# Moving batch 1's rounds, two tail steps and half of a weight cast in a hand-ordered attention and gated-MLP kernel

## The chip, the cores and the metric

The kernel runs on one core of a Trainium2 chip. The metric is the device time of one execution in microseconds. The times shown are medians over several runs of the same kernel; the profile is one execution, recorded by the hardware profiler.

The engines are named as in the profile: PE is TensorE, DVE VectorE, ACT ScalarE, POOL GpSimd, SP SyncE. Each works through its own list of instructions in order. PEld is TensorE's weight load. SPq and ACTq are transfers issued from SP's and ACT's queues.

## The reference

Attention over 8 batches, 8 heads, 576 positions and a head size of 64, with a mask in blocks of 64, followed by a gated two-layer network on all 4608 rows:

```python
scores = scale * np.matmul(q, k.transpose(0, 1, 3, 2))
mask = (pos[:, None] // 64) >= (pos[None, :] // 64)
scores = np.where(mask, scores, -1e9)
attn = softmax(scores)                        # over the last axis
attn_out = np.matmul(attn, v)                 # (8, 8, 576, 64)
x = attn_out.transpose(0, 2, 1, 3).reshape(4608, 512)
out = (np.maximum(x @ w_gate, 0) * (x @ w_val)) @ w_out   # 512 -> 1536 -> 512
```

Inputs and output are float32 in device memory. The kernel multiplies in bf16.

## The kernel before

**Two streams of TensorE work.** Each batch's 512 main positions are one tile of the network; the last 64 positions of all batches (the tails) make a ninth tile. For one tile the generator `ffn_gen` issues 144 products of 128 x 128 by 128 x 512, one at a time: for each of 12 blocks of the hidden layer four products for the gate and four for the value (positions 0 to 95), then 48 for the output. Tiles 0 and 1 take some of these in another order, and tile 0 splits its output: eight blocks into two partial sums, which DVE copies out (L645), and the last four added later (L656). ACT makes `gate_sb` from the gate (L578), DVE multiplies it by the value into `hT` (L583), DVE copies the outputs (L659), and ACT's queue stores them (L554).

Between these products stands the attention of the next batch. A batch has four rounds, one per pair of heads; round r belongs to batch r // 4. A round has scores (`visit`, L378), exponentials on ACT (L387 and L393) into `attnT`, zeroed corners for the mask (`corners`, L686), a product with v for each head (`head_av` or `both_av`, L491), a normalisation on DVE (L456, L457) into `xnat`, and a transpose into `xT`, either on TensorE (`to_xT_pe`, L537 and L538) or as a transfer from SP (`to_xT_dma`, L543). The tail of a batch has the same steps in `tail_at`, ending in `xtail` and a transfer into `xTt` (L485).

**Order.** Everything is in `manual_schedule`: each engine executes its instructions in the order in which the Python code issues them. `run(base, events)` sorts pairs of a position and a function, advances the generator to that position and then calls the function. So an event's position fixes where its instructions stand on every engine and in every queue. Tile 0's events have base 0, tile 1's base 144; `round_at` turns one line of positions into the events of a round. Because a queue is a list in program order, an instruction that has to wait keeps all behind it waiting.

**Batches 0 to 3 come in by float32 transfers.** SP issues loads into ten buffers named `stage`; POOL, DVE or ACT casts them to bf16. Weights come the same way (`load_w_out` and `cast_w` for `wo`, L323). The class `Early` holds these steps for one batch: `cast_qk` (L168), `cast_v` (L181), `cast_v_chunks` (L189), `cast_v_tail` (L195), `cast_tails` (L178, the last 64 positions of q and k into `q_bt` and `k_bt`). q and k must then be transposed:

- batch 1 on TensorE: `pe_mains(hp)` for the four pairs of heads (L238, with copies into `qTm` and `kTm` by DVE and ACT, L244), and `pe_tails` for the tails (L256 and L262, into `qTt` and `kTt`);
- batches 2 and 3 by transfers from SP: `transpose(hg)` into `perm` (L209), and `transpose_tails` (L217). `unpermute` (L223) copies `perm` into place on DVE and POOL.

`q_bt` and `k_bt` have two buffers each. Batch 3's `cast_tails` writes the pair that batch 1's `pe_tails` reads.

**PSUM.** Most products share three buffers named `ffnp`; `one` has one and `sc` two. A new tile of such a pool waits for the reader of the tile that had its buffer. `pe_mains` takes one `ffnp` buffer for q and one for k, and so do gate, value, heads, `to_xT_pe` and the output tiles.

**The steps around the change, with their times in the profile.** In tile 0 (its end, 36 to 66 us) batch 1 passes through casts, `pe_mains` and rounds 4 to 7; the last of the 12 wo blocks come in as `w_out[2]`, two pieces of two blocks each, the first cast by POOL, the second by DVE. In tile 1 (66 to 104 us) rounds 8 to 11 of batch 2 run, with SP's queue carrying, in this order: batch 0's `xTt`, batch 3's loads (`load_3`), batch 2's tail transposes, xT of round 8, two `perm` transposes of batch 3's first half, xT of rounds 9 and 10, two `perm` transposes of its second half, xT of round 11, batch 3's tail transposes.

POOL's order there is written by `mains_3`, which is called for the two halves of batch 3 in turn:

```python
        def mains_3(h0):
            early[3].cast_qk(h0, 4, (pool, pool))
            if h0 == 0:
                early[3].cast_tails((pool, pool))
```

Of the kernel before, what the change touches and what calls it, by code (L numbers as in the profile page):

```python
# [17 lines left out]
def kernel(  # L18
# [299 lines left out]
    def load_w_out(i):  # L318
        return load_w(wo[i], moe_w_out, 512 * i)

    def cast_w(sts, eng):
        for dst, st in sts:
            eng(dst, st)  # L323
# [40 lines left out]
    def visit(r):  # L364

        b, hp = divmod(r, 4)
        at = attnT[r % 4]
        first = psum_sc.tile([128, 2, 512], FP, name="sc")
        second = psum_sc.tile([128, 2, 512], FP, name="sc")
        third = thirds()  # L370
        for c, hh in [(c, hh) for c in (2, 0, 1, 3) for hh in range(2)]:
            where = {
                0: first[:, hh, :],
                1: second[:, hh, 0:384],
                3: second[:, hh, 384:512],
                2: third[hh],
            }
            nc.tensor.matmul(  # L378
                where[c].rearrange("p (c n) -> p c n", n=128),
                kTm[b % 2][head_of(hh), c, hp, :],  # L380
                qTm[b % 2][head_of(hh), c:4, hp, :],
                start=True,
                stop=True,
            )

        def exp(sc, lo):
            return lambda: nc.scalar.activation(  # L387
                at[:, :, lo : lo + 512], sc, AF.Exp, scale=scale
            )

        def exp_third():
            for hh in range(2):
                nc.scalar.activation(  # L393
                    at[:, hh, 1024:1280], third[hh], AF.Exp, scale=scale
                )

        return exp_third, exp(first, 0), exp(second, 512)
# [44 lines left out]
    def corners(r, zero):  # L442

        at = attnT[r % 4]
        for lo, n in ((0, 512), (896, 128)):
            two = at[64:128, :, lo : lo + 2 * n].rearrange("p g (c n) -> p g c n", c=2)
            zero(two[:, :, :, 0:64])
# [52 lines left out]
    def head_av(r, hh):  # L500
        b, hp = divmod(r, 4)
        h = 2 * hp + hh
        at = attnT[r % 4]
        if hh == 0:
            xnats[r] = sb.tile([128, 4, 128], BF, name="xnat", bufs=3)
        xnat = xnats[r]
        if b > 0 or hh == 1:
            av = psum_ffn.tile([128, 4, 65], FP, name="ffnp")
        else:
            av = psum_one.tile([128, 4, 65], FP, name="one")  # L510
        products_with_v(b, h, at[:, hh, :], av)
        normalise(xnat[:, :, 64 * hh : 64 * hh + 64], av)

    def both_av(r):

        b, hp = divmod(r, 4)
        xnats[r] = sb.tile([128, 4, 128], BF, name="xnat", bufs=3)
        for hh in range(2):
            sc = psum_sc.tile([128, 2, 512], FP, name="sc")
            av = sc[:, 0, 0:260].rearrange("q (p e) -> q p e", e=65)  # L520
            products_with_v(b, 2 * hp + hh, attnT[r % 4][:, hh, :], av)
            normalise(xnats[r][:, :, 64 * hh : 64 * hh + 64], av)
# [160 lines left out]
    dve, act, pool = nc.vector.tensor_copy, nc.scalar.copy, nc.gpsimd.tensor_copy  # L683
# [7 lines left out]
    with tc.manual_schedule(engines={E.PE, E.DVE, E.Activation, E.Pool, E.SP}):  # L691
# [57 lines left out]
        e1, e2 = Early(1), Early(2)  # L749
        e1.load_qk(0, 4)  # L750
        ffn(23)
        w_out = [load_w_out(i) for i in range(2)]
# [12 lines left out]
        cast_w(w_out[1], pool)  # L765
        e1.cast_v(0, 4, pool)
        cast_w(w_out[2][:1], pool)
        e1.cast_qk(4, 4, (pool, None))
        e1.cast_v(4, 4, pool)
        e0.cast_tails((pool, pool))  # L770
# [12 lines left out]
        def round_at(p, r, av, to_xT, after=(6, 13)):  # L783

            exps = []

            def begin():
                exps.extend(visit(r))
                exps[0]()
                exps[1]()  # L790

            return [
                (p, begin),
                (p + after[0], lambda: exps[2]()),
                (min(p + after[1], av[0] - 0.5), lambda: corners(r, zero_dve)),
                *(
                    [(av[0], lambda: both_av(r))]
                    if av[1] is None
                    else [(av[i], lambda i=i: head_av(r, i)) for i in range(2)]
                ),  # L800
                (to_xT[0], lambda: to_xT[1](r)),
            ]

        def tail_at(p, b, av):
            exps = []
            x = sb.tile([64, 512], BF, name="xtail", bufs=2)

            def begin():
                exps.extend(tail_visit(b))
                exps[0]()  # L810
                exps[1]()

            def end():
                tail_av(b, 1, x)
                tail_to_xT(b, x)

            return [
                (p, begin),
                (p + 6, lambda: exps[2]()),
                (av[0], lambda: tail_av(b, 0, x)),  # L820
                (av[1], end),
            ]
# [25 lines left out]

        def mains_3(h0):
            early[3].cast_qk(h0, 4, (pool, pool))  # L850
            if h0 == 0:
                early[3].cast_tails((pool, pool))

        def v_3():
# [8 lines left out]
        def mains_2(h0):  # L863
            e2.load_v_chunks(h0 // 4)
            e2.cast_qk(h0, 4, (pool, pool))
            e2.transpose(h0 // 4)

        def load_tails():
# [2 lines left out]
            e2.load_tails((0, 1))  # L871
            e2.load_tails((2,))

        events = round_at(101, 4, (113, 114), (117, pe_xT), (6, 11))
        events += round_at(108, 5, (120, 120.1), (128, pe_xT), (6, 11.5))
        events += round_at(128.5, 6, (139, 140), (146, pe_xT), (4, 9))
        events += round_at(138, 7, (148, None), (153, pe_xT), (3, 8))
        events += [
            (80, lambda: e1.cast_qk(0, 4, (None, dve))),
            (96, lambda: e1.pe_mains(0, (dve, act))),  # L880
            (98, lambda: e1.pe_mains(1, (dve, act))),
            (112.3, lambda: cast_w(w_out[2][1:], dve)),
            (120.2, lambda: e1.cast_qk(4, 4, (None, act))),
            (123, lambda: e1.pe_mains(2, (dve, act))),
            (125.5, lambda: e1.pe_mains(3, (dve, act))),
            (128, lambda: mains_2(0)),
            (142, lambda: e0.pe_tails((dve, act))),
            (143, lambda: mains_2(4)),
# [3 lines left out]
        events = tail_at(24, 0, (40, 44)) + tail_at(116, 1, (132, 136))  # L892
        for r, p in ((8, 41), (9, 58), (10, 75), (11, 92)):
            events += round_at(p, r, (p + 21, p + 25), (p + 25, to_xT_dma))
        events += [
            (100, lambda: e1.pe_tails((dve, act))),
            (20, lambda: store.pop()()),
            (25, un(2, 0, (dve, pool))),
            (28, un(2, 1, (dve, pool))),
# [3 lines left out]
            (56, un(2, 3, (dve, pool))),  # L903
            (60, tails_2),
            (66, lambda: mains_3(0)),
            (81, lambda: early[3].transpose(0)),
            (82, lambda: mains_3(4)),
            (101, lambda: early[3].transpose(1)),
            (118, lambda: early[3].transpose_tails()),
# [5 lines left out]
        for b in range(3, B):  # L915
            events = tail_at(120, b, (136, 140))
# [43 lines left out]
```

## Time and profile before

| | before |
|---|---|
| median of 7 runs | 374.36 us (373.0 to 376.07) |
| the profiled execution, its own time | 373.0 us |
| its span, first to last instruction | 370.8 us |
| PE busy | 357.0 us (96%) |
| DVE, ACT, POOL busy | 173.9, 169.8, 111.1 us |
| granted TensorE clock | 0.995 of full speed |
| moved by transfers | 51.35 MB, 138 GB/s |

PE's idle time by stretch, from the windows view:

| stretch, us | PE busy, us | PE idle, us |
|---|---|---|
| 0 to 20 | 16.39 | 3.61 |
| 20 to 40 | 19.96 | 0.04 |
| 40 to 60 | 17.95 | 2.05 |
| 60 to 80 | 19.84 | 0.16 |
| 80 to 100 | 19.74 | 0.26 |
| 100 to 120 | 16.76 | 3.24 |
| 120 to 140 | 19.95 | 0.05 |
| 140 to 160 | 19.27 | 0.73 |

In a line of the profile, the tile written stands left of the arrow and the tile read right of it; L numbers are lines of the kernel. A line of the timeline gives start, length, engine, line, operation, tiles and a count; brackets at its end give the idle time of the engine just before it and what ended that time. A line of the waits gives total, count and longest, in us. In the slices each digit is a fortieth of the span in tenths of busy time.

### The profile page before, as it was taken

The page shows a single profiled execution, that of the slowest core. Times are in us where ns is not written, and L with a number is a line of the kernel's source. Part 1 is how long each engine was busy: PE and PEld are TensorE (multiplying, and loading weights), DVE is VectorE, ACT ScalarE, POOL GpSimd, SP SyncE. Part 2 cuts the span into 40 slices and gives each one's busy share as a digit, 9 for nine tenths or more (in the row PEclk, how much of TensorE's full clock was granted, in tenths as well). Part 3 has the DMA queues.
Part 4 walks back from the last instruction along what each step waited for, and adds up shares of the span by engine and source line. Part 5 has one row for each costly group of instructions (what it writes and reads, how often), then busy time and mean ns, then how long its engine had stood idle before and what let it go on. Part 6 is the DMA issues. An engine that isn't in the chain of part 4 may idle for free.

```text
span 370.8 us, 7469 instructions
## 1 busy us (share of the span) xinstructions
PE 357.0 (96%) x2963; PEld 176.9 (48%) x2963; DVE 173.9 (47%) x399; ACT 169.8 (46%) x278; POOL 111.1 (30%) x141
## 2 busy tenths in 40 slices
PE   6999989999969999999999999999999999999996
PEld 2644445445534545444554455444544454444443
DVE  4744475675534644454345533554354443423432
ACT  4833646667335662456445544553465323302310
POOL 6675635282379920940066004000000000000000
PEclk9899999999999999999999999999999999999999
DMA  8999999999879999997499857875200320020014
GB/s 256 292 348 360 297 244 325 206 214 248 133 156 119 128 131 181 166 125 147 110 95 134 122 128 85 53 80 135 80 17 14 63 82 7 0 87 28 0 36 108
DMA packets 145187, 51.35 MB, mean 138 GB/s; under 512 B 124544, under 2 KB 139136, under 8 KB 145152
## 3 DMA queue, kind: packets, MB, share of 16 engines
q1 hardware_dynamic: 83616, 34.62, 43.8%
q0 software_dynamic: 56256, 7.08, 40.7%
q10 hardware_dynamic: 5280, 9.18, 7.7%
q8 instruction: 23, 0.38, 0.5%
q14 instruction: 12, 0.10, 0.1%
HBM read 37.75 MB, written 9.44 MB: 127 GB/s over the span
## 4 chain that ended last, share of the span: by engine, by line
PE 86%; DMA 6%; DVE 3%; ACT 3%; issue 1%; POOL 1%; SPq 0%; ACTq 0%; DVEq 0%; POOLq 0%
PE ffnp L568 49%; PE ffnp L625 21%; PE ffnp L491 4%; DMA xT<-xnat 3%; PE sc L378 3%; PE ffnp L471 2%; DMA perm<-k_bf 2%; PE one L378 1%; PE ffnp L238 1%; DMA perm<-q_bf 1%; PE ffnp L679 1%; PE sc L335 1%; PE sc L412 1%; ACT gate_sb L578 1%; DVE hT L583 1%
## 5 line engine op out<-in xcount | busy, mean ns | idle before, releaser
L583 DVE TENSOR_TENSOR hT<-gate_sb,ffnp 128x512 bf16<-128x512 bf16 x106 | 72.7, 686 | 95.5 <-PE ffnp L568 82.6
L578 ACT ACTIVATE gate_sb<-ffnp 128x512 bf16<-128x512 f32 x108 | 64.7, 601 | 105.9 <-PE ffnp L568 105.7
L568 PE MATMUL ffnp<-xT,wg 128*128 128x512 bf16 x384 | 103.9, 380 | 4.4 <-DMA xT<-xnat 3.9
L625 PE MATMUL ffnp<-wo,hT 128*128 128x512 bf16 (+1 forms) x444 | 102.5, 374 | 0.7 <-DVE hT L583 0.4
L568 PE MATMUL ffnp<-xT,wv 128*128 128x512 bf16 x376 | 100.2, 380 | 0.0
L568 PEld LDWEIGHTS <-wv 128*128 128x128 bf16 x432 | 39.9, 98 | 49.3 <-issue 5.7
L568 PEld LDWEIGHTS <-wg 128*128 128x128 bf16 x432 | 40.2, 98 | 47.6 <-issue 5.0
L625 PEld LDWEIGHTS <-hT 128*128 128x128 bf16 x444 | 40.5, 98 | 42.0 <-issue 1.3
L387 ACT ACTIVATE attnT<-sc 128x1024 bf16<-128x1024 f32 x56 | 56.9, 1041 | 0.0
L659 DVE COPY ob<-ffnp 128x512 f32<-128x512 f32 (+1 forms) x35 | 23.7, 676 | 40.1 <-PE ffnp L625 40.1
L276 POOL DMA_DIRECT2D v_bf<-in_v_dram x20 | 16.8, 879 | 68.8 <-PE ffnp L471 68.8
L491 PEld LDWEIGHTS <-attnT 128*128 128x128 bf16 x640 | 26.1, 98 | 15.1 <-DVE xnat L457 3.5
L456 DVE RECIPROCAL recip<-ffnp 128x4 f32<-128x4 f32 (+1 forms) x73 | 13.0, 179 | 32.9 <-PE ffnp L491 21.0
L491 PE MATMUL ffnp<-v_bf,attnT 128*128 128x65 bf16 x570 | 26.6, 194 | 0.8 <-DVE attnT L686 0.8
L393 ACT ACTIVATE attnT<-one 128x256 bf16<-128x256 f32 x28 | 10.7, 384 | 32.4 <-PE ffnp L378 29.3
L457 DVE TENSOR_TENSOR xnat<-ffnp,recip 128x256 bf16<-128x256 f32 x57 | 24.2, 424 | 2.5 <-DMA xT<-xnat 0.6
L433 ACT ACTIVATE attnTt<-one 64x256 bf16<-64x256 f32 x8 | 3.0, 377 | 34.0 <-PE ffnp L412 32.6
L378 PE MATMUL sc<-qTm,kTm 64*128 64x512 bf16 (+1 forms) x168 | 17.2, 305 | 0.2 <-ACT attnT L387 0.2
L378 PEld LDWEIGHTS <-kTm 64*128 64x128 bf16 x224 | 9.3, 94 | 16.2 <-issue 12.3
L424 ACT ACTIVATE attnTt<-sc 128x1024 bf16<-128x1024 f32 x16 | 15.6, 1016 | 0.0
L276 POOL DMA_DIRECT2D k_bf<-in_k_dram x16 | 14.3, 932 | 0.7 <-DMA v_bf<-in_v_dram 0.4
L276 POOL DMA_DIRECT2D q_bf<-in_q_dram x16 | 14.4, 953 | 0.0
(87 smaller groups left out, 260.3 us busy)
## 6 DMA issues: line engine op xcount, KB each, us to landing
out_dram<-ob ACTq DMA_DIRECT2D x32, 256.0 KB, 2.8
stage<-in_moe_w_gate_dram SPq DMA_DIRECT2D x6, 512.0 KB, 9.1
stage<-in_moe_w_val_dram SPq DMA_DIRECT2D x6, 512.0 KB, 8.8
stage<-in_q_dram SPq DMA_DIRECT2D x6, 512.0 KB, 6.5
stage<-in_k_dram SPq DMA_DIRECT2D x6, 512.0 KB, 7.6
stage<-in_moe_w_out_dram SPq DMA_DIRECT2D x6, 512.0 KB, 9.2
stage<-in_v_dram SPq DMA_DIRECT2D x20, 128.0 KB, 5.4
stage<-in_v_dram SPq DMA_DIRECT2D x8, 256.0 KB, 6.5
```

The costliest lines, as they stand in the source:

```text
L276: nc.gpsimd.dma_start(dst, src[b, :, 128 * c : 128 * c + n, :].rearrange("h p d -> p h d"),)
L378: nc.tensor.matmul(where[c].rearrange("p (c n) -> p c n", n=128), kTm[b % 2][head_of(hh), c, hp, :], qTm[b % 2][head_of(hh), c:4, hp, :], ...
L387: return lambda: nc.scalar.activation(at[:, :, lo : lo + 512], sc, AF.Exp, scale=scale)
L424: return lambda: nc.scalar.activation(at[:, :, 2 * i : 2 * i + 2, 0:256], main[i].rearrange("p g (h n) -> p g h n", h=2), AF.Exp, scale=scale,
L456: nc.vector.reciprocal(recip, av[:, :, 64])
L457: nc.vector.tensor_tensor(out=out, in0=av[:, :, 0:64], in1=recip.to_broadcast([rows, n, 64]), op=AX.mult,)
L491: nc.tensor.matmul(av[:, p, :], at[:, col : col + 128], v_bf[b % 2][:, c, h, :], start=(p == 0), stop=(c == p), skip_group_check=True,)
L568: nc.tensor.matmul(to, (wg, wv)[t][f // 4][:, c, 128 * (f % 4) : 128 * (f % 4) + 128], x[:, c], start=(c == 0), stop=(c == 3),)
L578: nc.scalar.activation(gate_sb, gate, AF.Relu)
L583: nc.vector.tensor_tensor(out=h, in0=gate_sb, in1=val, op=AX.mult)
L625: nc.tensor.matmul(op, hT[f][:, 128 * s : 128 * (s + 1)], wo[f // 4][:, f % 4, n0:n1], start=(f == lo), stop=(f == hi - 1),)
L659: nc.vector.tensor_copy(ob, op)
```

## The change

It has three parts.

1. In tile 1 batch 1's `pe_tails` stands at position 88 instead of 100, and batch 3's `cast_tails` follows the casts of its second half instead of its first. SP's order of transfers stays the same.
2. In tile 0 `pe_mains(0)` and `pe_mains(1)` move from 96 and 98 to 93 and 95, round 4 begins at 96 instead of 101 and round 5 at 104 instead of 108. Round 4's corners are zeroed at 107 instead of 112, its heads stand together at 112, and its xT at 116. Round 5's heads move from 120, ahead of `pe_mains(2)` and `pe_mains(3)`, to 127, behind them, and its xT from 128 to 131, behind the scores of round 6. `pe_mains(3)` moves from 125.5 to 125.
3. The last piece of wo (two blocks, 1024 columns) is cast in halves: one block by POOL, ahead of the cast of batch 1's second half of q, and one by DVE, between the normalisations of round 4's two heads.

```diff
         cast_w(w_out[2][:1], pool)
+        last_w = [[a[:, c : c + 1] for a in w_out[2][1]] for c in range(2)]
+        cast_w(last_w[:1], pool)
         e1.cast_qk(4, 4, (pool, None))
...
         def mains_3(h0):
             early[3].cast_qk(h0, 4, (pool, pool))
-            if h0 == 0:
+            if h0 == 4:
                 early[3].cast_tails((pool, pool))
...
-        events = round_at(101, 4, (113, 114), (117, pe_xT), (6, 11))
-        events += round_at(108, 5, (120, 120.1), (128, pe_xT), (6, 11.5))
+        events = round_at(96, 4, (112, 112.1), (116, pe_xT), (6, 11))
+        events += round_at(104, 5, (127, 127.1), (131, pe_xT), (6, 15))
         events += round_at(128.5, 6, (139, 140), (146, pe_xT), (4, 9))
         events += round_at(138, 7, (148, None), (153, pe_xT), (3, 8))
         events += [
             (80, lambda: e1.cast_qk(0, 4, (None, dve))),
-            (96, lambda: e1.pe_mains(0, (dve, act))),
-            (98, lambda: e1.pe_mains(1, (dve, act))),
-            (112.3, lambda: cast_w(w_out[2][1:], dve)),
+            (93, lambda: e1.pe_mains(0, (dve, act))),
+            (95, lambda: e1.pe_mains(1, (dve, act))),
+            (112.05, lambda: cast_w(last_w[1:], dve)),
             (120.2, lambda: e1.cast_qk(4, 4, (None, act))),
             (123, lambda: e1.pe_mains(2, (dve, act))),
-            (125.5, lambda: e1.pe_mains(3, (dve, act))),
+            (125, lambda: e1.pe_mains(3, (dve, act))),
...
         events += [
-            (100, lambda: e1.pe_tails((dve, act))),
+            (88, lambda: e1.pe_tails((dve, act))),
             (20, lambda: store.pop()()),
```

## Prediction

> **What bounds the kernel now.** I read the busy line and the slices first, then the waits, then the chain, then the timeline of the two stretches that the change touches.
>
> ```profile
> PE 357.0 (96%) x2963; PEld 176.9 (48%) x2963; DVE 173.9 (47%) x399; ACT 169.8 (46%) x278; POOL 111.1 (30%) x141
> PE   6999989999969999999999999999999999999996
> PE ffnp L568 <- DMA xT<-xnat: 3.9, 3, 3.2
> POOL q_bt L178 <- PE ffnp L256: 7.0, 1, 7.0
> ```
>
> TensorE is busy for 357.0 of 370.8 us. From 160 us to 320 us the windows show it busy without a gap, so only its holes can be won: 3.6 us in the first 20 us and 3.8 us in the last 51 us (neither touched), 2.05 us between 40 and 60 us (tile 0's end), and 3.24 us between 100 and 120 us. The last is one wait, the first product of tile 2 that needs round 11's block of xT. The change works on both middle holes. The 7.0 us for which POOL waits on batch 1's tail transposes is what its tile 1 half takes away, so the question is whether that wait leads to the 3.24 us. The timeline answers (start, length, engine, line):
>
> ```profile
> 75.72 0.42 DVE L457 TENSOR_TENSOR xtail<-ffnp,recip 64x256 bf16<-64x256 f32 x1
> 76.16 1.58 SPq L485 DMA_TRANSPOSE xTt<-xtail  x1
> 94.72 1.03 POOL L168 CAST k_bf<-stage 128x1024 bf16<-128x1024 f32 x1
> 95.38 1.26 SPq L209 DMA_TRANSPOSE perm<-q_bf  x1
> 96.73 1.28 SPq L209 DMA_TRANSPOSE perm<-k_bf  x1
> 98.11 4.38 SPq L543 DMA_TRANSPOSE xT<-xnat  x2
> 102.59 1.26 SPq L209 DMA_TRANSPOSE perm<-q_bf  x1
> 103.94 2.19 SPq L209 DMA_TRANSPOSE perm<-k_bf  x1
> 106.23 1.63 SPq L543 DMA_TRANSPOSE xT<-xnat  x1
> 109.41 0.38 PE L568 MATMUL ffnp<-xT,wg 128*128 128x512 bf16 x1 [3.24 <-DMA xT<-xnat]
> ```
>
> The transposes at 95.38 and 96.73 take batch 3's first half, cast by 85.58. Those at 102.59 and 103.94 take the second half, which POOL finished at 95.75, 6.8 us before SP came to it. SP had no free moment: from 71.98 to 107.86 its instructions follow each other within about 0.13 us. The last xT block was ready at 98.47 (DVE) and stood in that queue until 106.23. So the hole comes from the queue, not from POOL. The chain of waits does run through POOL's casts, but there it joins the cast that ends at 95.75 to the transpose issued at 96.73, which takes the other half.
>
> What starts this queue matters more. SP finishes its previous load at 76.04; the transpose at 76.16 waits for DVE's xtail, which ends at 76.14. So SP alone could start 0.12 us sooner, no more, while any delay of TensorE before tile 1's position 44 delays xtail, this transpose and, in order, all that follows up to 109.41. Time won before position 44 only lengthens the hole; time lost there reaches the end.
>
> **Part 1, batch 3's tail casts and batch 1's tail transposes.** Order on SP is unchanged. On POOL the two second-half casts come ahead of the two tail casts, and pe_tails moves from position 100 to 88, from 92.23 to about 88.1. The second-half loads were issued at 80.31 and 81.03; with the page's medians of 6.5 and 7.6 us they land near 86.8 and 88.6, so the casts (1.03 us each) end near 89.6 and the tails (0.61 each) near 90.8. Waiting behind them are the copies of perm at 102.48, held by a landing, and on SP the second-half transposes at 102.59 and the tail transposes at 107.95. All keep over 6 us of cover, and no later load waits for the stage buffer that the tails give back later. Gain 0. On TensorE the same eight transposes run (0.4 us); their evacuations (DVE 0.28, ACT 0.37) now stand before a gate copy and round 11's exponentials, worth perhaps 0.2 us, under the 3.24 us hole. Without the hole it would cost that 0.2.
>
> A rule would read this differently. The row: a 128x1024 bf16 transpose (256 KB) is issued in 1.26 to 2.19 us and lands in 3.7 to 5.6. The Trainium skill, page "DMA: Bandwidth & Descriptors", section "Latency and other measured facts", gives DMA transposes about 261 GB/s: 1.0 us for that block, and for the 1.66 MB from 89.96 to the last xT an estimate of 6.4 us. By the rule that queue would be empty at 96.4, POOL's cast at 95.75 would set the second-half transposes, xT would follow at 98.5 and there would be no hole; a delay in tile 0 would still pass. By the trace it takes 19.4 us. The 3.2 us row decides for the trace.
>
> **Part 2, tile 0.** What holds TensorE here:
>
> ```profile
> 47.82 0.48 PE L491 MATMUL ffnp<-v_bf,attnT 128*128 128x65 bf16 x10 [0.82 <-DVE attnT L686]
> 49.17 1.04 POOL L168 CAST q_bf<-stage 128x1024 bf16<-128x1024 f32 x1 [2.92 <-DMA stage<-in_q_dram]
> 51.73 1.04 ACT L168 CAST k_bf<-stage 128x1024 bf16<-128x1024 f32 x1 [0.93 <-DVE recip L456]
> 52.84 0.40 PE L238 MATMUL ffnp<-ident,k_bf 128*128 128x128 bf16 x4 [0.20 <-ACT k_bf L168]
> 58.01 0.28 PE L378 MATMUL one<-qTm,kTm 64*128 64x256 bf16 x1
> ```
>
> I followed the new order with the durations of these rows: a 512-column product 0.215 us, four transposes 0.22, a head's ten products 0.30, a round's scores 0.65, DVE's evacuation 0.69, ACT's 0.59, about 0.45 from a product's start to its reader.
>
> Pulling pe_mains(0), (1) and rounds 4 and 5 forward adds waits: 0.4 us at the first k transposes (their PSUM buffer is that of the last gate, whose copy ends at 39.51) and 0.2 at the next. It removes the 0.41 us wait at 40.59, and the 0.82 at 47.82, since the corners of round 4 are now zeroed before the two ob copies. Round 4's first head comes to 46.3 instead of 47.82. Then come three waits on DVE of about 0.4 each (for the second ob copy, for DVE's half of the wo cast, for the second head's product), and the q transposes of pe_mains(2) come to 50.8 instead of 52.25.
>
> There the lead ends. k_bf's second half lands at 50.74 (issued 42.94, 7.8 us to landing). Ahead of its cast ACT issues an out store; before, that store waited for a later load and left at 51.33. Now it waits for this landing. So the cast runs from about 51.2 to 52.24 and the k transposes start at 52.3, against 52.84: TensorE waits 1.3 us, and of a lead of 1.5 about 0.5 is left.
>
> After it, round 5's two heads (0.6 us), which stood before this gate and beside its wait, stand behind it. From these transposes to the end of round 6's scores the new order holds 0.22+0.43+0.22+0.22+0.43+0.60+0.22+0.65 = 2.99 us of work, and 0.6 of waits (0.2 on the evacuation that also held the old order, 0.1 at the heads, 0.3 on round 5's DVE products): 55.95 against 55.74. Four transposes and ten products follow (2.37 against 2.15), so round 7 starts at 58.4 against 58.01: **0.4 us late**. Nothing from there to 76.14 gives it back: TensorE idles 0.16 us from 60 to 80. xtail, SP's queue and the last xT move by 0.4 at most. Bounds: -0.5 (the lead at the gate is kept, worth only 0.1 at the end) and +1.3 (the lead is all lost and each reader costs 0.2 more). I take +0.4, the walk's own sum.
>
> **Part 3, the last wo piece.** DVE's cast of 1024 columns takes 0.69 us. Halved, it lies between 0.35 and 0.69 on DVE; on POOL between 0.52 (half of 1.04) and 0.61 (the 128x512 cast of k_bf takes 613 ns). I take 0.4 and 0.61, by the nearest rows. The piece lands at 46.6, so POOL casts from 46.6 to 47.2 within its 2.92 us of idle time before 49.17. The q_bf cast does not move unless that cover is gone; then it would cost 0.61. DVE's half now falls between the normalisations of round 4's heads, near 48.0. It holds one wo product, the second head's product on DVE and to_xT of round 4, all ahead of the 1.3 us wait at the gate: 0. With that wait gone, about 0.3.
>
> The second rule speaks against splitting. DVE's perm copies take 0.55 us each at 99.15, with POOL idle, and 1.01 at 68.69, beside POOL's copies. The Trainium skill, page "SBUF — State Buffer", section "Who interferes with whom", says that a DVE cast in a two-port mode and GpSimd lock each other out for a whole instruction. By the rule, halves that meet cost DVE up to 0.61 us, still under the gate's 1.3. By the rows' times they miss each other by 0.8 us. Both give 0.
>
> **Sum.** 0 + 0.4 + 0 = +0.4 us on the profiled execution: its span of 370.8 becomes 371.2 and its 373.0 us (2.2 lie outside the span) 373.4. The seven runs' median is 1.36 us above that execution, so I forecast 374.36 + 0.4 = 374.8 us. About 0.3%, 1.1 us, is what a measurement of this kernel can tell from no change.
>
> **Rivals.**
> (a) The walk is right, or its lead survives: the end moves by -0.1 to +1.1 us; 374.3 to 375.4. For it: the hole absorbs gains and the gate absorbs the first half of tile 0. Chance 0.62.
> (b) POOL did hold SP, as the chain view has it: with the casts sooner the hole of 3.24 us goes in part or whole; 371.1 to 373.2. Against it: SP came to the second half 6.8 us after its cast. Or the queue's pace differs from run to run so that the hole opens less. Chance 0.10.
> (c) Slower: ACT works in order, and round 5's xT copy (0.59 us) now stands between round 6's two large exponentials (1.0 each). Round 7's second scores need the later one's PSUM buffer. If round 6's scores are later than 56.1 this holds TensorE; each further 0.1 us is then paid again in round 7's exponentials and at its corners, 0.4 to 1.0 us on top of the 0.4, all of it handed to xtail. It passes the bound once xtail ends after 77.3. 375.5 to 376.2, likeliest 375.7. For it: ACT is in use for 13.45 of the 20 us from 40 to 60. Against it: in my walk the exponential ends at 58.65, just before the scores ask for it at 58.75. Chance 0.28.
>
> That the change does not do what it says is excluded by the order of the instructions: each named move is there.
>
> **Numbers.** 0.62 + 0.28 + 0.10 = 1. The range leaves out most of (b) and the end of (c): 373.5 to 376.1.
>
> **What would show it.** Right: POOL's 7.0 us wait gone or under 3; SP's second-half transposes again over 25 us after the xTt transpose; a wait of 3 us or more on xT at tile 2's start; k transposes of pe_mains(2) near 52.3; round 7's scores at 58.2 to 58.7; the corner wait gone. Wrong: the xT wait under 2 us (then b), xtail later than 77.3 (then c), or k_bf's cast no sooner than before.

## The result, and the profile after

The changed kernel takes 374.12 us (median of 27 runs, 371.47 to 377.14), the kernel before 374.46 us (median of 64 runs, 372.44 to 376.67). The ratio, taken over the runs within 1.5% of the fastest of their kernel and not the quotient of these medians, is 0.9999, with a 95% interval of 0.9984 to 1.0014: no difference that these runs can tell. The forecast was 374.8 us, 0.4 us over the median that stood on record then, and under the 1.1 us that it took for the least that can be told.

The profiled execution of the changed kernel took 375.76 us (span 373.7), 2.8 us more than the profiled execution before, although the medians are equal. First its busy time, then the row of granted clocks in 40 slices, then the two longest waits of TensorE in the middle of the kernel.

```profile
PE 361.3 (97%) x2963; PEld 178.1 (48%) x2963; DVE 174.1 (47%) x399; ACT 169.6 (45%) x278; POOL 111.8 (30%) x142
PEclk9999999999987999999999999999999999999999
...
PE ffnp L568 <- DMA xT<-xnat: 2.9, 1, 2.9
PE ffnp L238 <- ACT k_bf L168: 1.5, 1, 1.5
```

TensorE's wait for xT is still there, 2.9 us in place of 3.2, and the gate at batch 1's k has become a wait of 1.5 us. The clock row shows what the median hides: two slices at 8 and 7 tenths, around the hole's end and behind it. The timeline of the hole's queue, after (start, length, engine, line):

```profile
77.18 0.42 DVE L457 TENSOR_TENSOR xtail<-ffnp,recip 64x256 bf16<-64x256 f32 x1
77.63 1.20 SPq L485 DMA_TRANSPOSE xTt<-xtail  x1
89.76 1.04 POOL L168 CAST k_bf<-stage 128x1024 bf16<-128x1024 f32 x1 [0.87 <-PE ffnp L568]
...
102.50 1.52 SPq L209 DMA_TRANSPOSE perm<-q_bf  x1
105.54 2.37 SPq L543 DMA_TRANSPOSE xT<-xnat  x1
...
110.48 0.59 PE L568 MATMUL ffnp<-xT,wg 128*128 128x512 bf16 x1 [2.86 <-DMA xT<-xnat]
```

POOL now ends the cast of batch 3's second half of k at 90.80 instead of 95.75. SP comes to its transposes at 102.50 all the same, 11.7 us later, and xT of round 11 is issued at 105.54. The hole ends at 110.48. The queue's unbroken stretch again begins with the transpose of xTt, 0.03 us after xtail's end at 77.60.

What made this execution longer is seen in the windows over the hole (TensorE's busy time stands first; the three last columns are granted clock, transfer share and GB/s):

```profile
108.00:110.00 2.00, 0.00 (x0) 0.00 (x0) 0.00 (x0) 0.80 (x1) 0.00 (x0) 0.87 1.21 190
110.00:112.00 2.00, 1.52 (x4) 0.55 (x4) 0.00 (x0) 0.90 (x2) 1.64 (x2) 0.50 0.28 49
112.00:114.00 2.00, 2.00 (x6) 0.73 (x5) 0.69 (x1) 0.62 (x1) 2.00 (x3) 0.50 0.65 53
114.00:116.00 2.00, 2.00 (x7) 0.60 (x5) 0.00 (x0) 0.60 (x1) 2.00 (x4) 0.50 1.73 110
...
112.00:114.00 2.00, 2.00 (x28) 1.29 (x27) 0.69 (x1) 0.75 (x2) 2.00 (x3) 1.00 1.68 124
```

TensorE is granted half its clock from before the hole's end to about 116.3 us; the last line is the same stretch of before, at full clock. From 110.48 on that is 5.8 us at half speed (to the 0.92 of the window from 116 to 118), or 2.9 us lost. With the 1.07 us by which tile 2's work goes on later (110.48 against 109.41), less the 0.73 us of idle time that before had between 140 and 160 us and this execution did not, it makes 3.2 us; the spans differ by 2.9, so 0.3 us of the sum is not accounted for.

Tile 0's gate, after:

```profile
52.41 1.04 ACT L168 CAST k_bf<-stage 128x1024 bf16<-128x1024 f32 x1 [1.99 <-DMA stage<-in_k_dram]
53.51 0.40 PE L238 MATMUL ffnp<-ident,k_bf 128*128 128x128 bf16 x4 [1.54 <-ACT k_bf L168]
59.67 0.28 PE L378 MATMUL one<-qTm,kTm 64*128 64x256 bf16 x1
```

This execution was already 0.79 us late at the last value products of tile 0 (L568 with `wv`, first at 39.50 against 38.71), ahead of all that the change moves. Batch 1's second half of k landed near 51.9 us instead of 50.7: it was issued at 43.01 and took 8.9 us, before 42.94 and 7.8. From the k transposes to round 7's scores it takes 6.16 us.

### The profile page after: what moved, and what is told of

Same layout as the page of the kernel before. It is cut to its first block, busy times and chain, and to the rows that moved or that the text cites. A ratio compares the mean times of both kernels' runs of the same rounds, so it can differ in the third digit from the quotient of the medians.

```text
span 373.7 us, 7467 instructions
## 1 busy us (share of the span) xinstructions
PE 361.3 (97%) x2963; PEld 178.1 (48%) x2963; DVE 174.1 (47%) x399; ACT 169.6 (45%) x278; POOL 111.8 (30%) x142
## 4 chain that ended last, share of the span: by engine, by line
PE 84%; DMA 11%; ACT 2%; POOL 1%; issue 0%; DVE 0%; SPq 0%; ACTq 0%; POOLq 0%
PE ffnp L568 45%; PE ffnp L625 23%; DMA stage<-in_moe_w_val_dram 5%; PE ffnp L491 4%; PE sc L378 3%; DMA stage<-in_moe_w_out_dram 3%; PE ffnp L471 3%; DMA stage<-in_k_dram 2%; PE one L378 1%; DMA xT<-xnat 1%; ACT attnT L351 1%; PE sc L412 1%; PE ffnp L679 1%; PE ffnp L238 1%; PE sc L335 0%
## 5 line engine op out<-in xcount | busy, mean ns | idle before, releaser
L568 PE MATMUL ffnp<-xT,wg 128*128 128x512 bf16 x384 | 104.9, 383 | 3.2 <-DMA xT<-xnat 2.9
L568 PE MATMUL ffnp<-xT,wv 128*128 128x512 bf16 x376 | 102.3, 385 | 0.0
L568 PEld LDWEIGHTS <-wv 128*128 128x128 bf16 x432 | 40.3, 98 | 49.6 <-issue 7.2
L568 PEld LDWEIGHTS <-wg 128*128 128x128 bf16 x432 | 40.4, 98 | 48.2 <-issue 6.6
L223 POOL COPY kTm<-perm 128x512 bf16<-128x512 bf16 x8 | 9.3, 1181 | 19.5 <-DMA perm<-k_bf 13.8
```

The costliest lines, as they stand in the source:

```text
L568: nc.tensor.matmul(to, (wg, wv)[t][f // 4][:, c, 128 * (f % 4) : 128 * (f % 4) + 128], x[:, c], start=(c == 0), stop=(c == 3),)
```

## The experiments

All were compared with the kernel before on the same chip; its medians in the four groups were 374.5 (runs 1 to 4), 374.8 (5 to 8), 374.54 (9 to 11) and 374.65 us (12). The theory to be tested was the prediction's: the hole is made by SP's queue, so part 1 is worth nothing, what happens in TensorE's order ahead of xtail passes through whole, and tile 0's gate eats the lead. The rivals were that POOL's 7.0 us wait makes the hole, and that the tile 0 order is worth more, either way, than the walk gave.

| run | kernel | median, us | ratio to before, 95% | runs at granted clock 0.994 or less |
|---|---|---|---|---|
| | before (all four groups) | 374.5 to 374.8 | | 66 of 134 |
| | after | 374.12 | 0.9999, 0.9984 to 1.0014 | 15 of 27 |
| 1 | before, second-half transposes later | 372.78 | 0.9947, 0.9923 to 0.9971 | 0 of 14 |
| 2 | after, the same | 372.12 | 0.9945, 0.9919 to 0.9971 | 0 of 10 |
| 3 | part 1 alone | 374.79 | 1.0011, 0.9989 to 1.0033 | 10 of 14 |
| 4 | parts 2 and 3 alone | 374.24 | 0.9992, 0.9972 to 1.0012 | 14 of 22 |
| 5 | before, work ahead of xtail | 377.32 | 1.0065, 1.0037 to 1.0092 | 2 of 7 |
| 6 | before, the same work behind it | 371.93 | 0.9939, 0.9918 to 0.9960 | 1 of 18 |
| 7 | run 1, batch 4's transposes earlier | 370.23 | 0.9878, 0.9841 to 0.9914 | 0 of 6 |
| 8 | run 2, round 5's heads first | 372.37 | 0.9936, 0.9911 to 0.9962 | 5 of 15 |
| 9 | run 2, batch 4's transposes earlier | 370.07 | 0.9887, 0.9855 to 0.9918 | 2 of 6 |
| 10 | part 3 alone | 374.22 | 1.0004, 0.9985 to 1.0023 | 7 of 22 |
| 11 | run 9, round 5's heads first | 370.06 | 0.9882, 0.9856 to 0.9908 | 1 of 6 |
| 12 | run 6 with half the work | 374.05 | 0.9981, 0.9957 to 1.0006 | 9 of 22 |

**Runs 1 and 2: take the queue out of the way.** The two transposes of batch 3's second half move on SP behind xT of round 11, in the kernel before and in the changed one. Their copies, which read the result, move to tile 2.

```diff
-            (101, lambda: early[3].transpose(1)),
+            (118, lambda: early[3].transpose(1)),
...
-                events.append((2, un(3, 2, (dve, pool))))
+                events.append((20, un(3, 2, (dve, pool))))
```

> The kernel before with one reordering in SP's queue: the two perm transposes of batch 3's second half stand behind xT of round 11 (position 118 of tile 1 instead of 101), and their unpermute at position 20 of tile 2 instead of 2. Queue theory: xT of round 11 is issued at about 102.6 us instead of 106.2 and lands near 105.7, before TensorE asks for it at 106.2; the wait of 3.2 us on xT at tile 2's start falls under 0.5 us and the time falls by 2.5 to 3.5 us, ratio 0.991 to 0.993. POOL theory (POOL's wait on batch 1's tail transposes holds the queue): POOL's casts end where they did, so the hole stays near 3 us and the ratio is 1.000.

> The changed kernel with the same reordering. Queue theory: the hole is gone here too, and with it the mask over tile 0: what tile 0's new order costs is now seen whole, so this is slower than the kernel before with the reordering by what the walk gave, 0.4 us (ratio to before 0.992 to 0.994). If tile 0's new order had gained time that the hole swallowed, this is the faster of the two, by up to 1 us.

Measured: 372.78 and 372.12 us. In the first, POOL's wait on the tail transposes has kept its full length (from the waits on POOL), while the three xT blocks of rounds 9 to 11 leave SP one behind the other (from the timeline):

```profile
POOL q_bt L178 <- issue: 7.0, 1, 7.0
...
98.78 4.91 SPq L543 DMA_TRANSPOSE xT<-xnat  x3
```

Tile 2's product with round 11's xT starts in run 1 without a wait:

```profile
106.94 0.39 PE L568 MATMUL ffnp<-xT,wg 128*128 128x512 bf16 x1
```

So the hole of 3.24 us is gone in both profiles: the queue made it, and POOL's wait did not. The gain of 2.0 us by the ratio (1.7 by the medians) is under the forecast 2.5 to 3.5 us, since a part moved on: at tile 3's start, 147 to 150 us, run 1 waits three times for xT, 1.7 us in all against 0.6 before, and the granted clock falls to 0.57 from 150 to 154 us. The two kernels differ only by the change under study, and their intervals lie on each other: with the hole gone it still brings and costs nothing that can be told. The 0.4 us by which run 2 was to be the slower does not show, and these intervals do not exclude it.

**Runs 3 and 4: the halves of the change.** Run 3 has part 1 alone (the tails), run 4 parts 2 and 3 alone (tile 0 and the wo halves); so each takes over some lines of the change and leaves the others as they were:

```diff
-            if h0 == 0:                                   # run 3
+            if h0 == 4:
-            (100, lambda: e1.pe_tails((dve, act))),
+            (88, lambda: e1.pe_tails((dve, act))),
...
-        events = round_at(101, 4, (113, 114), (117, pe_xT), (6, 11))       # run 4, and so on
+        events = round_at(96, 4, (112, 112.1), (116, pe_xT), (6, 11))
```

> The kernel before with the two tail steps of tile 1 alone (pe_tails at 88, batch 3's cast_tails after the second half's casts). Queue theory: POOL's wait of 7.0 us goes, the second-half casts end near 89.6 instead of 95.75, SP issues the second-half transposes at 102.6 as before and the hole stays at 3.2 us: ratio 1.000, within 0.001. POOL theory: the hole shrinks by 2 us or more, ratio 0.994 or less.

> The changed kernel with the two tail steps of tile 1 put back: tile 0's new order and the split wo cast alone. The walk: POOL's wait of 7.0 us back, round 7's scores 0 to 0.6 us later than before relative to the landing of the second half of k, ratio 1.000 to 1.002. If the new order gained and the gain was given back by the tail steps, the ratio is 0.998 or less.

Measured: 374.79 and 374.24 us, both the same as before within 0.3%. The first product of tile 2 in run 3, and the gate of tile 0 in run 4:

```profile
109.57 0.38 PE L568 MATMUL ffnp<-xT,wg 128*128 128x512 bf16 x1 [3.32 <-DMA xT<-xnat]
```

```profile
51.74 0.40 PE L238 MATMUL ffnp<-ident,k_bf 128*128 128x128 bf16 x4 [1.42 <-ACT k_bf L168]
57.91 0.28 PE L378 MATMUL one<-qTm,kTm 64*128 64x256 bf16 x1
```

Run 3 has no wait of POOL on the tail transposes, and the hole is 3.32 us: part 1 does what it says, and it is worth nothing. Run 4 has the gate's 1.42 us, and 6.17 us from there to round 7. Its round 7 starts 7.76 us after the landing of k's second half (issued at 43.05, 7.1 us to landing), against 7.27 before: 0.5 us later, as forecast.

**Runs 5 and 6: the same work ahead of the queue's start and behind it.** `junk(10)` issues ten products of 512 columns that nobody reads, about 2.15 us of TensorE (10 x 0.215). Run 5 puts them at position 31 of tile 1, ahead of xtail; run 6 at position 61, behind it.

```diff
         events += [
+            (31, lambda: junk(10)),      # run 5;  run 6: (61, ...)
             (100, lambda: e1.pe_tails((dve, act))),
```

> The kernel before with ten 512-column matmuls of no use (about 2.15 us of PE) at tile 1's position 31, ahead of batch 0's tail (its xtail is written at position 44). Queue theory: SyncE's unbroken stretch begins with that tail's transpose, so it and the 3.2 us hole of round 11's xT move along with PE: hole again 3.0 to 3.5 us, transpose of xTt some 2 us later than in before, and the whole loses all of it: +2.1 us, 376.3 to 376.8 beside 374.5, ratio 1.005 to 1.006. Rival (the hole's end is set by something that does not follow PE, a load or GpSimd's chain): the hole takes the 2.1 us up and shrinks to about 1.1 us, ratio 0.999 to 1.001. Third (the lost time is the clock's, not the wait's): ratio anywhere, the hole unchanged, and the granted clock decides.

> The same ten matmuls at tile 1's position 61, behind that tail. Queue theory: SyncE has begun its stretch already and does not wait for PE in it, so the 2.1 us are taken from the hole: 1.0 to 1.4 us of it left, ratio 0.999 to 1.001 (374.1 to 374.9). It is the test of the prediction's statement that between the tail and tile 2 PE's gains and losses are worth nothing. Rival (the hole follows PE, since round 9's or 10's xnat is what SyncE waits for): hole 3.2 us still, ratio 1.005 to 1.006 as for the other.

Measured: 377.32 us, 0.65% slower, and 371.93 us, 0.6% faster, for the same added work. Run 5's queue start and hole:

```profile
79.16 1.65 SPq L485 DMA_TRANSPOSE xTt<-xtail  x1
...
112.34 0.38 PE L568 MATMUL ffnp<-xT,wg 128*128 128x512 bf16 x1 [2.77 <-DMA xT<-xnat]
```

xTt left 3.0 us later than in before and the end of the hole came 2.9 us later: what TensorE loses ahead of xtail passes to the end. (2.15 us of the 3.0 are the added work; this execution was also 1.2 us late at round 7, ahead of it.) That is the prediction's rule, and the rival (a hole whose end stands still) is out. Run 6 went further than any of the theories stated for it. In its profile no wait for xT is left at all:

```profile
100.00:120.00 20.00, 20.00 (x213) 10.46 (x210) 12.36 (x25) 8.89 (x15) 16.90 (x20) 1.00 1.49 145
```

The time from the start of xTt's transfer to TensorE going on with round 11's xT is the measure of the queue. It was 33.25 us in before (76.16 to 109.41), and lies between 32.85 and 35.33 us in the seven profiles that have the hole. With 33.25 and TensorE's arrival 32.0 us after xTt (75.71 to 107.70), 1.25 us of hole should have been left, as forecast. In run 6 the block was there when TensorE arrived, so the queue needed under 32.0 us. The median suggests that this was the rule in its runs. An estimate: without any wait for xT there run 7 below took 370.23 us, and with 2.15 us more that makes 372.4; 1.25 us of hole would have made 373.6, and run 6 measured 371.9. Why SP's queue is quicker beside this work is not known.

**Run 12: half of it.** Five products in place of ten.

```diff
-            (61, lambda: junk(10)),
+            (61, lambda: junk(5)),
```

> The sixth experiment with five of the ten matmuls (about 1.1 us of PE at tile 1's position 61). In the sixth the hole went altogether and the kernel came out 1.5 to 3.1 us faster with 2.1 us more work, where the queue theory alone had it equal. Clock theory (a wait of PE of about 3 us is followed, in near half the runs, by a stretch at a lower granted clock, which costs some 1.5 us in such a run): the hole shrinks to about 2.1 us, no run or few below a granted clock of 0.995, and the time falls by the mean cost of the dips, 0.6 us: 373.7 to 374.2, ratio 0.997 to 0.999. Queue theory alone: 374.3 to 374.7, ratio 1.000. Third (SyncE's stretch itself gets 2 us shorter when PE comes later): hole gone, ratio 0.990 to 0.993.

Measured: 374.05 us; 9 of its 22 runs had a granted clock of 0.994 or less. Its hole:

```profile
111.15 0.38 PE L568 MATMUL ffnp<-xT,wg 128*128 128x512 bf16 x1 [4.25 <-DMA xT<-xnat]
```

Here the queue took 35.33 us, the longest of all: the last xT, issued at 105.74, let TensorE go only 5.4 us later (3.2 in before). So the third theory, a queue that is always quicker when TensorE comes later, does not hold in this profile. Nor did the clock theory's hole of 2.1 us and its "no run or few" come: 9 of 22 runs are at the lower clock, about the share of before. The ratio's interval takes in the forecasts of the clock and of the queue. The run does not decide why run 6 gained more than its sum; what it shows is that the hole is no constant of the kernel: 2.8 to 4.3 us in the seven profiles that have it.

**Runs 7, 9 and 11: take away the next wait as well.** In run 1 SP stood idle from about 115 to 122 us, and then batch 4's four transposes (from 123.4 to 137.3) held the xT blocks of rounds 13 to 15. Run 7 issues these four at position 44 of tile 2, ahead of round 12's xT. Run 9 has the same two queue edits on the changed kernel. Run 11 also puts round 5's heads and xT back ahead of `pe_mains(2)`, by the edit of run 8 below.

```diff
-                events.append((66, lambda b=b: dma_transposes(b + 1)))
+                events.append((44 if b == 3 else 66, lambda b=b: dma_transposes(b + 1)))
```

> The kernel before with batch 3's second-half transposes at tile 1's position 118 (the first experiment), and with batch 4's transposes at tile 2's position 44 in place of 66, so ahead of round 12's xT on SyncE. Queue theory: SyncE stood idle from about 115 to 122 us there, and batch 4's four transposes then held round 13's and 14's xT until 137; issued sooner, they leave the queue free sooner, and the 1.7 us of waits for xT at 147 to 151 us go: 371.0 to 372.2, ratio 0.991 to 0.994. Rival (batch 4's rows have not landed by then, so SyncE waits for them with round 12's xT behind it): the waits stay at 1.5 us or more, 372.5 to 373.5.

> The changed kernel with the two queue edits that took the waits for xT away (batch 3's second-half transposes at tile 1's position 118, batch 4's transposes at tile 2's position 44): no wait for xT is left to hide what the change does to tile 0 and to the tails. Prediction's steps (tile 0 +0.4 us, tails and halves 0): 370.2 + 0.4 = 370.6, range 369.9 to 371.3, ratio to before 0.987 to 0.991, no wait for xT of over 0.5 us, granted clock 0.995 or above. Rival (the hole had hidden a gain of the change): 368.9 to 369.8, ratio under 0.987. Other rival (it had hidden a loss): 371.5 or more.

> The changed kernel with those two queue edits and round 5's heads ahead of batch 1's second half (the order of the eighth experiment). Prediction's step that the heads behind the gate cost 0.4 to 1.0 us of tile 0: 0.4 to 1.0 us under the ninth run, 369.5 to 370.2, ratio 0.985 to 0.988, PE busy 18.4 us or more in 40 to 60. Rival (order there is worth nothing): equal to the ninth run within 0.3 us.

Measured: 370.23, 370.07 and 370.06 us, 1.1 to 1.2% faster than before. In run 7 batch 4's first transpose leaves at 117.01 in place of 123.39, and all four xT blocks of batch 3 start from 130.06:

```profile
117.01 4.67 SPq L286 DMA_TRANSPOSE qTm<-q_bf  x1
...
130.06 11.51 SPq L543 DMA_TRANSPOSE xT<-xnat  x4
```

TensorE is then busy for 39.95 of the 40 us in the windows from 100 to 120 and from 140 to 160. Run 7 came out 0.8 us faster than its forecast's lower end (371.0). That forecast took 1.7 us of waits off run 1; run 1's profile also has 3.4 us at half clock at tile 3's start, worth up to 1.7 us, which run 7's has not. That these are the 0.8 us is likely, not shown. Run 9 answers the question that the hole had kept open: with no wait for xT to hide behind, the change again makes no difference (0.9887 against 0.9878, intervals nearly the same). Neither rival of run 9 came, though two of its six runs had a clock under the 0.995 that it was to keep; a tile 0 effect of 0.4 us is below what these intervals tell. Run 11's 370.06 us fits both its forecast (369.5 to 370.2) and its rival (run 9 within 0.3 us), so the time does not decide. Its sign failed: TensorE is busy for 16.66 us between 40 and 60, not 18.4 or more, because a product waited 1.96 us for POOL (run 10 below).

**Run 8: round 5's heads ahead of the gate.** On the kernel of run 2:

```diff
-        events += round_at(104, 5, (127, 127.1), (131, pe_xT), (6, 15))
+        events += round_at(104, 5, (120, 120.1), (122.5, pe_xT), (6, 15))
```

> The changed kernel with the second-half transposes at position 118 (the second experiment), and with round 5's two heads and its xT back ahead of batch 1's second half (tile 0's positions 120, 120.1 and 122.5 in place of 127, 127.1 and 131). Prediction's step: with the heads behind the gate round 7's scores come 6.1 us after the k transposes of pair 2; with them ahead of it the gate's wait falls from 1.5 us to under 0.6, and round 7 comes 5.0 to 5.4 us after them, so 0.4 to 1.0 us of tile 0 is won: 371.2 to 371.9, ratio 0.991 to 0.994. Rival (PE is filled anyway and the order there is worth nothing): within 0.1% of the second experiment, 371.8 to 372.5.

Measured: 372.37 us, beside 372.12 of run 2: nothing won that can be told. Its ratio of 0.9936 lies in the forecast's range and also within 0.1% of run 2's, so the time does not decide; the trace says more. The order did as expected on the spot: the wait on k's cast is gone, and round 7's scores (58.59) come 4.94 us after the k transposes (53.65). But these now stand behind the heads and xT, with a wait of 0.51 us for DVE's xnat and 0.23 for ACT's copy of xT ahead of them, and round 7 starts no sooner than in the other profiles of either order (57.4 to 59.7). In this profile the work was only moved to the other side of the gate.

**Run 10: the wo halves alone.** The kernel before with part 3.

```diff
+        last_w = [[a[:, c : c + 1] for a in w_out[2][1]] for c in range(2)]
+        cast_w(last_w[:1], pool)
...
-            (112.3, lambda: cast_w(w_out[2][1:], dve)),
+            (112.3, lambda: cast_w(last_w[1:], dve)),
```

> The kernel before with the last wo piece's second part cast in two halves, one on GpSimd and one on VectorE, and nothing else of the change. Prediction's step: hidden, 0: ratio 0.998 to 1.002, 374.0 to 375.2, the hole of 3 us as in before. Rival (GpSimd's cast in tile 0 delays batch 1's k cast or VectorE's order at the gate): +0.4 to +0.8 us, ratio 1.001 to 1.002, not to be told by the time, but k's transposes of pair 2 in tile 0 would wait 0.4 us or more longer than in before (0.2 us there).

Measured: 374.22 us, ratio 1.0004. Its gate in tile 0 waited all the same, and in run 11 a product waited for POOL's half:

```profile
53.85 0.40 PE L238 MATMUL ffnp<-ident,k_bf 128*128 128x128 bf16 x4 [1.56 <-ACT k_bf L168]
```

```profile
49.03 0.59 PE L625 MATMUL ffnp<-wo,hT 128*128 128x512 bf16 x2 [1.96 <-POOL wo L323]
```

The time says 0, as forecast. The sign that its rival named does show, a gate wait of over 0.4 us. But what released ACT's cast of k there, at 52.75, was the landing of k itself, 9.1 us after its issue and after 2.46 us of waiting, not POOL or DVE, and run 7, which has no halves, waited 0.54 us at this gate. So the halves did not delay the cast; the late landing did.

## Why the prediction was right

**The hole (the first term, 0).** Shown. The queue makes it: moving two transposes out of its way took the hole away with POOL's wait untouched (run 1); removing POOL's wait left 3.32 us (run 3). Work ahead of xtail passes on (run 5), work behind it does not (runs 6 and 12). One statement was too strict: that xtail starts the queue. In ten of the fourteen profiles xTt leaves within 0.12 us of xtail's end. In runs 3, 9, 10 and 11 SP's own last load ended later, and xTt left 0.46, 1.19, 1.07 and 1.26 us after xtail; a delay of TensorE up to that size would have passed nothing on there. Run 9, whose xtail ended at 76.36:

```profile
75.53 1.92 SPq L158 DMA_DIRECT2D stage<-in_v_dram  x1
77.55 1.23 SPq L485 DMA_TRANSPOSE xTt<-xtail  x1
```

The trace's pace of SP's transposes was the right one to use. The Trainium skill's "DMA: Bandwidth & Descriptors", section "Latency and other measured facts", with its 261 GB/s, would have had no hole by the prediction's estimate; in the eight profiles with this order SP took 27.9 to 30.3 us from xTt to the issue of round 11's xT.

**Tile 0 (the term of +0.4).** The corner wait and the hT wait are gone in all profiles of the change's order (after and runs 2, 4 and 9). Run 9 tests the walk best, since its execution comes to tile 0's end as the one before did: the last value products start at 38.71 in both, and k's second half lands near 50.7 in both (42.83 + 7.9 and 42.94 + 7.8). Before, and then run 9:

```profile
38.71 1.03 PE L568 MATMUL ffnp<-xT,wv 128*128 128x512 bf16 x4
```

```profile
38.71 0.38 PE L568 MATMUL ffnp<-xT,wv 128*128 128x512 bf16 x1
52.27 0.40 PE L238 MATMUL ffnp<-ident,k_bf 128*128 128x128 bf16 x4 [1.25 <-ACT k_bf L168]
58.44 0.28 PE L378 MATMUL one<-qTm,kTm 64*128 64x256 bf16 x1
```

The walk had the k transposes at 52.3 after a wait of 1.3 us and round 7 at 58.4; measured are 52.27, 1.25 and 58.44, against 58.01 before: +0.43 us, by the mechanism that was named. The parts were less exact. Waits that were put at 0.4 us came out at 0.17 to 0.28. The written terms (52.3 + 2.99 + 0.6 + 2.37) make 58.26, so 58.4 holds 0.14 us that are not named.

But +0.4 belongs to that execution and is no constant. Where the gate waits (after, runs 4 and 9), the new order starts round 7 between 7.7 and 7.8 us after k's landing. Run 2 came to its last value products at 41.00, k was there, and round 7 started at 59.38, 18.38 us later. The old order needs 19.25 or 19.26 us for the same way in runs 3, 5, 6 and 12, and 19.30 before. So the new order is the longer one where k lands late beside TensorE, and the shorter one, by 0.9 us in this single profile, where it does not. On average over the profiles, from the first of these products to round 7, the old order (before and runs 1, 3, 5, 6, 7, 10, 12) and the new one (after and runs 2, 4, 9) both take 19.5 us. An average effect of tile 0 on the time is therefore not shown. The landing is what the walk took as fixed: it took 6.6 to 9.1 us from issue, in no clear relation to the order.

**Part 3 (0).** Right in the time (run 10). The reason given was too good: the piece "lands at 46.6" in one execution, but in run 11 both halves waited for it until about 48.1 and a product waited 1.96 us for POOL's. Round 7 came there 20.61 us after the first of the last value products, against 19.07 us in run 8, which has the same order in tile 0. These 1.5 us passed nothing on, since xtail still ended (76.42) before SP's last load (77.58). The halves were to miss each other, and by 0.75 us they do in the profile after. They met in runs 9 and 11, and the one that started later was the longer: 0.70 us for DVE's in run 9 and 0.87 for POOL's in run 11, against 0.42 and 0.61 after.

**The rivals and the signs.** (b), POOL: refuted by runs 1 and 3. Its second half, a pace of the queue that differs from run to run, did show: the hole measures 2.8 to 4.3 us, and the profile of run 6 has none. (c), ACT's order: its sign in tile 0, a wait of round 7's second scores for ACT, is in none of the four profiles with the new order. Of the six signs of being right, the profile after has two, POOL's wait and the corner wait gone. Four missed: SP's second-half transposes came 24.9 us after xTt (over 25), the hole was 2.86 us (3 or more), the k transposes stood at 53.51 (near 52.3) and round 7 at 59.67 (58.2 to 58.7). Two signs of being wrong occurred: xtail at 77.60, and k's cast at 52.41, no sooner than before (51.73). The signs of the k transposes, of round 7, of xtail and of k's cast fit this execution's late start (0.79 us) and late landing of k (1.2 us), more than the order: run 9 has 52.27, 58.44, 76.36 and 51.17. So the signs were set too narrowly for single executions.

**What the number shows.** Little by itself: the interval of the ratio is -0.6 to +0.5 us and holds 0 as well as +0.4. The forecast holds because its mechanisms do, for the hole by experiment and for tile 0 by one matched profile; that the average came so near to no change is not something the walk of one execution could know.

**What the sum lacked.** It counted waits at their length. A wait of some 3 us here can also cost half of the following stretch (next section); this hit both kernels about alike, 66 of 134 runs and 15 of 27, so the forecast of the median survived. It also lacked how far the landing of k moves from execution to execution.

## What to carry to other kernels

Before a wait is worked on, ask which in-order queue ends last in it and where that queue starts: 7.0 us of POOL's waiting was worth nothing, and moving two transposes behind one in the SP queue was worth 2.0 us, with a second such move 4.6 us in all. Added work is a good probe: the same ten products cost 0.65% ahead of the point where the queue starts and cost nothing behind it. A walk through one profile gives the effect in that execution: before it is taken for the average, find what it holds fixed (here the landing of one load) and how far that moves. When one hole closes, look for the next one made by the same queue, and read the granted clock just after each hole, since the hole's price does not end with it.

## What was not expected of the hardware

**A wait of TensorE is followed, in some executions, by a stretch at half clock.** In two-microsecond windows the granted clock falls to 0.50 after the hole in five of the seven profiles that have it (after, runs 4, 5, 10 and 12), and after the waits at tile 3's start in runs 1, 2 and 8, where the windows cut it so that they read 0.50 to 0.58. Added up (the missing share of each window, divided by one half), it is 3.4 us at half clock each time, and 6.8 us in after and run 10. Before and run 3, with holes of 3.24 and 3.32 us, have none there. (Some profiles, before and run 9 among them, have such a stretch near 8 to 16 us too.) The runs' mean clocks show how often it comes: one such stretch takes 0.46% off the mean of a 371 us span, and 0.994 or less, so more than one, have 123 of the 248 runs of the kernels with the hole and 9 of the 75 runs of those without it (runs 1, 2, 6 to 9 and 11). In the runs of before these have medians 0.9 to 1.4 us above the others.

The Trainium skill's "TensorE: Matmul & The Clock Gate", section "Part 1: The HAM clock gate", has the rule: an idle window of about 3.4 us brings half clock, about as much activity lifts it, and the window runs freely, which would leave it to the execution whether a gap fills one. The 0.50, the 3.4 us and the element of chance agree with the traces. That only a gap of a full window would bring it does not: the holes of run 5 (2.77 us) and after (2.86 us) are shorter than 3.4 us, in run 1 the longest single wait was 1.0 us and three of them made 1.7 us within 3.1 us, and the clock fell each time.

**The pace of SP's transposes varies from execution to execution.** The same 21 transfers took 27.9 to 30.3 us from xTt to round 11's xT, and TensorE could go on 2.9 to 5.4 us after that one's issue. The size of a hole read from one profile is good to about 1 us.
